# Attention's wide exponential cut into 1536 and 512 columns, and the normalisation's VectorE steps moved one behind each score copy

## The chip, the cores and the metric

The kernel runs on one core of one Trainium2 chip. The time is the device time of one execution in microseconds (us); before the change it is 2981.12 us, the median of three runs (2979.9 to 2981.21). The core's engines run side by side and wait for one another by semaphores: TensorE (PE in the profile; PEld are its weight loads), VectorE (DVE), ScalarE (ACT), GpSimd (POOL) and SyncE (SP), which issues most DMAs.

## What is computed

Two kinds of layers take turns, each on a layer norm of x and added to x: a long convolution (S4) and attention. x is 2048 x 640, all in float32. The change touches attention alone, which has 32 heads of 20 channels, all with the same keys and values:

```python
q = (x @ wq).reshape(B, S, H, Dh)        # S 2048, H 32, Dh 20, heads moved ahead of rows
k = x @ wk
v = x @ wv
scores = einsum("bhqd,bkd->bhqk", q, k) * Dh ** -0.5
p = softmax(scores, axis=-1)
o = einsum("bhqk,bkd->bhqd", p, v)
y = o.reshape(B, S, H * Dh) @ wo
...
x = x + A(layernorm(x)); x = x + B(layernorm(x))
x = x + A(layernorm(x)); x = x + B(layernorm(x))
```

## The kernel before

`attn_layer` runs twice (layers b and d); nearly all of its time is `main_loop`, whose work is cut into 1024 tiles. A tile is 128 keys by 1024 columns: 256 queries of four heads. Tiles run over four blocks of 512 queries (nb), in each over eight groups of four heads (hg), in each over two halves of the queries (f) and 16 blocks of keys (t), so 32 tiles make one (nb, hg).

What happens to a tile:

- **scores** (L1298): two matmuls on TensorE into a PSUM tile of two banks, of which there are three (`ps2`, tag s2).
- **the exponential** on ScalarE, in one of two ways. A *direct* tile goes from PSUM to SBUF (pt, L1304, 1024 columns). Two tiles of six are put *aside*: VectorE copies their scores to SBUF (L1311, the score copy), two of them side by side in a tile pw, and ScalarE later takes both in one *wide* exponential of 2048 columns in place (L1429).
- **values** (L1321): matmuls with the values, the probabilities as moving data, which add up over the 16 blocks of keys in one PSUM bank (po). The values have a column of ones, so the softmax's denominators come out as a row of the same sums.

After 32 tiles VectorE *normalises*: it copies the bank to SBUF (on, L1347), transposes (L1336), takes the reciprocal of the denominators (L1337) and transposes back (L1338), and multiplies (L1352); then SP sends the parts of on to chunks ot of 128 channels (L1358). The banks for values are two, s10 and s11, and (nb, hg) uses the one of hg % 2. The other is free for the **projection** (L1393): one eighth of one chunk times wo, which VectorE adds to x (L1380). A layer has some 150 projections in the loop; they are let in by a credit of 0.52 per half cycle.

TensorE, ScalarE and VectorE work in the order in which the code is written (`tc.manual_schedule`), and DMAs in the order of their queue. The loop goes in cycles c of six tiles. A cycle first lets ScalarE take the wide exponential of tiles c and c + 1, then has two halves (h). Each half issues three scores (a *burst*: one direct, one aside, one direct), then one of VectorE's waiting pieces, then, in `behind`, the values of three tiles three to one places back and perhaps a projection. In the first half these are the last three direct tiles of the cycle before, in the second the two put aside and the first direct one. ScalarE's order in a cycle is so: wide, direct, direct, direct, direct.

The order before for the normalisation: the copy of the bank and the first transposition follow the last of the 32 tiles' values at once, in `behind`; the other two pieces come one each in the next two halves. In a half whose last tile is tile 0 or 1 of a new (nb, hg), there is no projection, since its bank is still being copied; a finished chunk's projections may start from tile 15 on.

Of the kernel before, what the change touches and what calls it, by code (L numbers as in the profile page):

```python
# [15 lines left out]
AF = mybir.ActivationFunctionType  # L16
# [19 lines left out]
SCALE = 20.0**-0.5  # L36
# [159 lines left out]
class Net:  # L196
# [1065 lines left out]
    def main_loop(self, ap, mp, kt, vt, nm, out):  # L1262
# [10 lines left out]
        tc, nc, qps = self.tc, self.nc, self.qps  # L1273
# [5 lines left out]
        def late_loads(late):  # L1279
            nc.gpsimd.memset(wol, 0.0)  # L1280
            for j in range(4):
                nc.gpsimd.dma_start(wol[32 * j : 32 * j + 20],
                                    self.ins["B_wo"][20 * (28 + j) : 20 * (29 + j)])
            if out is None:
                self.conv_weights(nc.gpsimd, late)
# [3 lines left out]
        queue, later = [], []  # L1289

        def scores(i):
            nb, hg, f, t = tiles[i]
            if (nb, hg) not in qps:
                self.load_q(ap, nm, nb, hg)
            sc = self.ps2(f"sc{nm}{i}")
            for par in range(2):
                rows = slice(64 * par, 64 * par + 62)
                nc.tensor.matmul(sc[:, 512 * par : 512 * par + 512], kt[rows, 128 * t : 128 * t + 128],  # L1298
                                 qps[nb, hg][rows, f].rearrange("p a c -> p (a c)"), start=True, stop=True)
            return sc  # L1300
# [12 lines left out]
        def values(i):  # L1313
            nb, hg, f, t = tiles[i]
            if (nb, hg) not in pos:
                pos[nb, hg] = self.ps1(f"po{nm}{nb}{hg}", hg % 2)
            po, pt = pos[nb, hg], pts.pop(i)

            for j in range(4):
                c0 = 512 * (j % 2) + 256 * (j // 2)  # L1320
                nc.tensor.matmul(po[32 * j : 32 * j + 32, 256 * f : 256 * f + 256], vt[:, t],  # L1321
                                 pt[:, c0 : c0 + 256], start=(t == 0), stop=(t == 15))

        def chunk(nb, k):
            if (nb, k) not in ots:
                ots[nb, k] = mp.tile([P, 512], F32, tag=f"ot{k}", bufs=2, name=f"ot{nb}{k}")
                if (nb, k) == (3, 4):

                    nc.gpsimd.memset(ots[nb, k], 0.0)
            return ots[nb, k]  # L1330

        def inverses(den, name):

            tr = mp.tile([P, 16, 32], F32, tag="tr", bufs=1, name=f"tr{name}")
            rc = mp.tile([P, 16], F32, tag="rc", bufs=2, name=f"rc{name}")
            steps = [lambda: nc.vector.transpose(flat(tr), den),  # L1336
                     lambda: (nc.vector.reciprocal(rc, tr[:, :, 20]),  # L1337
                              nc.vector.transpose(flat(tr), rc[:, :, None].to_broadcast([P, 16, 32])))]  # L1338
            return flat(tr), steps

        def flat(a):
            return a.rearrange("p a b -> p (a b)")

        def normalize(nb, hg):
            po = pos.pop((nb, hg))
            on = mp.tile([P, 512], F32, tag="on", bufs=2, name=f"on{nb}{hg}")
            nc.vector.tensor_copy(on, po)  # L1347
            inv, steps = inverses(on, f"{nb}{hg}")
            steps[0]()

            def finish():
                nc.vector.tensor_tensor(on, on, inv, ALU.mult)  # L1352
                for j in range(4):
                    r = 20 * (4 * hg + j)
                    while r < 20 * (4 * hg + j) + 20:
                        e = min(20 * (4 * hg + j) + 20, (r // 128 + 1) * 128)
                        o = 32 * j + r - 20 * (4 * hg + j)
                        nc.sync.dma_start(chunk(nb, r // 128)[r % 128 : r % 128 + e - r], on[o : o + e - r])  # L1358
                        r = e
                for k in range(80 * hg // 128, 80 * (hg + 1) // 128):  # L1360
                    later.extend((nb, k, u) for u in range(8))

            pieces.extend([steps[1], finish])

        def normalize_last():

            po = pos.pop((3, 7))
            inv, steps = inverses(po, "l")
            for call in steps:
                call()  # L1370
            on = mp.tile([P, 512], F32, tag="on", bufs=2, name="onl")
            nc.vector.tensor_tensor(on, po, inv, ALU.mult)
            return on
# [15 lines left out]
        def product(py, o, w, u, m, start, stop, c0=0, n=320):  # L1389
            i, half = u // 2, u % 2  # L1390
            c0 += 320 * half
            for j in range(0, P, m):
                nc.tensor.matmul(py[j : j + m], o[:, 128 * i + j : 128 * i + j + m], w[:, c0 : c0 + n],  # L1393
                                 start=start, stop=stop)

        def projection(hg):

            nb, k, u = queue.pop(0)
            py = self.ps1(f"py{nm}{nb}{k}{u}", 1 - hg % 2)[:, 0:320]
            product(py, ots[nb, k], wo[:, k], u, 32, True, True)  # L1400
            add(nb, u, py, k == 4)

        n = len(tiles)
        credit, pieces = [0.0], []

        def behind(group):

            for i in group:
                values(i)
                if i % 32 == 31 and i + 1 < n:  # L1410
                    normalize(*tiles[i][:2])
            if not group:
                return
            if group[-1] % 32 >= (15 if group[-1] < n - 32 else 8):
                queue.extend(later)
                later.clear()
            credit[0] = min(credit[0] + 0.52, 1.5)
            if queue and credit[0] >= 1 and group[-1] % 32 not in (0, 1):
                credit[0] -= 1
                projection(tiles[group[-1]][1])  # L1420

        with tc.manual_schedule(engines={mybir.EngineType.PE, mybir.EngineType.Activation,
                                         mybir.EngineType.DVE}):
            for i, put in ((0, direct), (6, aside), (1, direct)):
                put(i, scores(i))
            for c in range(0, n, 6):
                w = wide.pop(c // 6, None)
                if w is not None:
                    nc.scalar.activation(flat(w), flat(w), AF.Exp, scale=SCALE)  # L1429
                for h in range(2):  # L1430
                    burst = [(c + 2 + 2 * h, direct), (c + 7 + 5 * h, aside), (c + 3 + 2 * h, direct)]
                    for i, put in burst:
                        if i < n:
                            put(i, scores(i))
                    if pieces:
                        pieces.pop(0)()
                    if c == 36 and h == 0:
                        late_loads(pts[38])
                    behind([i for i in range(c - 3 + 3 * h, c + 3 * h) if 0 <= i < n])
            behind([n - 1])  # L1440
            on = normalize_last()
            if out is None:
                self.norm("c", 0)

            last = []
            for g in range(3):
                tile_ = self.ps2(f"pl{nm}{g}")
                last += [tile_[:, 0:320], tile_[:, 512:832]]
            last.append(self.ps1(f"pl{nm}6", 0)[:, 0:320])
            last.append(self.ps1(f"pl{nm}7", 1)[:, 0:320])  # L1450
            left = queue + later
            for u in range(8):
                items = [(ots[nb, k], wo[:, k]) for nb, k, v in left if v == u and k < 4]
                items.append((ots[3, 4], wo[:, 4]))
                for n, (o, w) in enumerate(items):
                    product(last[u], o, w, u, P, n == 0, False)
            for u in range(0, 8, 2):
                for v in (u, u + 1):
                    product(last[v], on, wol, v, P, False, True)
                for v in (u, u + 1):  # L1460
                    add(3, v, last[v], True)
# [83 lines left out]
```

## Time and profile before

| | us |
|---|---|
| median of three runs | 2981.12 |
| the profiled execution | 2978.3 |
| its span, first to last instruction | 2976.4 |
| attention loop of layer b, about | 729 to 1664 |
| attention loop of layer d, about | 2024 to 2958 |

| engine, whole span | busy us | share |
|---|---|---|
| TensorE | 2733.0 | 92% |
| ScalarE | 2414.1 | 81% |
| VectorE | 2027.1 | 68% |

The two loops are 1869 of the 2976 us. In the loops all three engines work at once, and an instruction's record in the profile can overlap with the next one's on the same engine: the durations of a group don't add up to the time that the engine needs, the distances between starts do. A row of the timeline is: start, us from start to end, engine, line, operation, what it writes and reads, shapes, count; in brackets the idle time before it and who ended that. In names pob and pod are banks of values in layers b and d, scb and scd their score tiles, pyb and pyd the projections' sums, pld the last products behind the loop. In a row of stages (from:to, length) stand the busy time and count of PE, PEld, DVE, ACT, POOL, then the granted TensorE clock, the DMA engines' share and GB/s.

### The profile page before, as it was taken

How to read it: one execution, taken by the hardware profiler on the slowest of the kernel's cores; microseconds unless marked ns; L12 is line 12 of the kernel's file. 1: busy time of each engine (PE TensorE's matmuls, PEld its weight loads, DVE VectorE, ACT ScalarE, POOL GpSimd, SP SyncE). 2: the span in 40 equal slices, each digit the busy share in tenths (PEclk: the TensorE clock that was granted, in tenths of full speed). 3: DMA queues.
4: the chain of work that ended last, by engine and by line, in shares of the span. 5: the costliest groups of instructions: out<-in, count | busy, mean ns of one | idle time of the engine just before them, and what ended most of it. 6: DMA issues, size and time to landing. Idle time of an engine off the chain costs nothing. (4 is left out here: it accounts for less than half of the span.)

```text
span 2976.4 us, 69802 instructions
## 1 busy us (share of the span) xinstructions
PE 2733.0 (92%) x29940; PEld 1570.6 (53%) x29940; DVE 2027.1 (68%) x2486; ACT 2414.1 (81%) x2565; POOL 84.9 (3%) x140
## 2 busy tenths in 40 slices
PE   2776989898999999999999998998999999999999
PEld 0333978775444444444444687774444444444444
DVE  7999899943566666666666699725566656666655
ACT  5888243454999999999999734338999999999997
POOL 0000001100000000000000011000000000000000
PEclk9655999998999999999999999999999999999999
DMA  6114555533200010101010256231001101110100
GB/s 146 34 17 103 183 167 114 139 104 104 82 23 27 22 26 22 28 21 28 23 27 20 88 114 161 65 128 43 22 27 31 35 23 32 35 28 23 44 20 24
DMA packets 144184, 178.81 MB, mean 60 GB/s; under 512 B 59524, under 2 KB 115844, under 8 KB 140244
## 3 DMA queue, kind: packets, MB, share of 16 engines
q1 hardware_dynamic: 119704, 141.90, 16.2%
q0 software_dynamic: 21872, 30.69, 5.6%
q8 instruction: 239, 3.92, 0.6%
q10 hardware_dynamic: 2288, 1.64, 0.2%
q14 instruction: 81, 0.66, 0.1%
HBM read 95.22 MB, written 48.04 MB: 48 GB/s over the span
## 5 line engine op out<-in xcount | busy, mean ns | idle before, releaser
L1304 ACT ACTIVATE pt<-scb 128x1024 f32<-128x1024 f32 x684 | 653.5, 1046 | 14.3 <-PE scb L1298 7.2
L1304 ACT ACTIVATE pt<-scd 128x1024 f32<-128x1024 f32 x684 | 652.5, 1044 | 12.7 <-PE scd L1298 7.2
L1429 ACT ACTIVATE pw<-pw 128x2048 f32<-128x2048 f32 x340 | 657.3, 1933 | 0.0
L1311 DVE COPY pw<-scd 128x1024 f32<-128x1024 f32 x340 | 415.4, 1222 | 218.1 <-PE scd L1298 215.0
L1311 DVE COPY pw<-scb 128x1024 f32<-128x1024 f32 x340 | 414.8, 1220 | 212.4 <-PE scb L1298 206.9
L1298 PE MATMUL scb<-qpb,kt 62*128 62x512 f32 x2048 | 378.6, 449 | 27.1 <-ACT pt L1304 17.7
L1298 PE MATMUL scd<-qpd,kt 62*128 62x512 f32 x2048 | 379.5, 449 | 24.4 <-ACT pt L1304 15.7
L1321 PE MATMUL pob<-pt,vt 128*32 128x256 f32 x5472 | 363.4, 383 | 0.1
L1321 PE MATMUL pod<-pt,vt 128*32 128x256 f32 x5472 | 362.9, 383 | 0.1
L1298 PEld LDWEIGHTS scb<-qpb,kt 62*128 62x128 f32 x2048 | 170.4, 186 | 260.9 <-ACT pt L1304 163.7
L1298 PEld LDWEIGHTS scd<-qpd,kt 62*128 62x128 f32 x2048 | 170.0, 185 | 259.7 <-ACT pt L1304 163.8
L1321 PEld LDWEIGHTS pob<-pt,vt 128*32 128x32 f32 x5472 | 160.6, 110 | 152.0 <-issue 63.9
L1321 PEld LDWEIGHTS pod<-pt,vt 128*32 128x32 f32 x5472 | 160.5, 110 | 152.0 <-issue 63.9
L1321 PE MATMUL pod<-pw,vt 128*32 128x256 f32 x2720 | 182.0, 385 | 1.0 <-DVE x L1380 1.0
L1321 PE MATMUL pob<-pw,vt 128*32 128x256 f32 x2720 | 182.0, 385 | 1.0 <-DVE x L1380 1.0
L1380 DVE TENSOR_TENSOR x<-pyd,x 128x320 f32<-128x320 f32 x149 | 72.6, 487 | 144.0 <-PE pyd L1393 144.0
L1380 DVE TENSOR_TENSOR x<-pyb,x 128x320 f32<-128x320 f32 x149 | 72.7, 488 | 141.0 <-PE pyb L1393 141.0
L1321 PEld LDWEIGHTS pob<-pw,vt 128*32 128x32 f32 x2720 | 71.1, 109 | 74.1 <-issue 42.4
L1321 PEld LDWEIGHTS pod<-pw,vt 128*32 128x32 f32 x2720 | 71.1, 109 | 73.3 <-issue 41.6
L1393 PE MATMUL pyb<-wo,ot 128*32 128x320 f32 x1192 | 107.5, 432 | 0.5 <-DMA ot<-on 0.5
L1393 PE MATMUL pyd<-wo,ot 128*32 128x320 f32 x1192 | 107.5, 432 | 0.4 <-DMA ot<-on 0.4
L654 PE MATMUL zc<-xnc,wf 128*128 128x256 f32 x384 | 87.4, 391 | 4.6 <-ACT xnc L821 4.5
(378 smaller groups left out, 3559.4 us busy)
## 6 DMA issues: line engine op xcount, KB each, us to landing
Akh<-kh SPq DMA_DIRECT2D x10, 2048.0 KB
kh<-Ak SPq DMA_DIRECT2D x5, 2048.0 KB
qhd<-qh SPq DMA_DIRECT2D x40, 256.0 KB
qld<-ql SPq DMA_DIRECT2D x40, 256.0 KB
qpb<-qhd SPq DMA_DIRECT2D x256, 40.0 KB
qpd<-qhd SPq DMA_DIRECT2D x256, 40.0 KB
ot<-on SPq DMA_DIRECT2D x216, 40.0 KB
wi<-in_c_wi SPq DMA_DIRECT2D x16, 512.0 KB
```

What stands on the lines that cost most here:

```text
L654: nc.tensor.matmul(zv[:, :, c, kk], self.wf[:, t + 4 * h, j, c, kk], x, start=(n == 0), stop=(n == 3))
L1298: nc.tensor.matmul(sc[:, 512 * par : 512 * par + 512], kt[rows, 128 * t : 128 * t + 128], qps[nb, hg][rows, f].rearrange("p a c -> p (a c) ...
L1304: nc.scalar.activation(pts[i], sc, AF.Exp, scale=SCALE)
L1311: nc.vector.tensor_copy(pts[i], sc)
L1321: nc.tensor.matmul(po[32 * j : 32 * j + 32, 256 * f : 256 * f + 256], vt[:, t], pt[:, c0 : c0 + 256], start=(t == 0), stop=(t == 15))
L1380: nc.vector.tensor_tensor(xh, py, xh, ALU.add)
L1393: nc.tensor.matmul(py[j : j + m], o[:, 128 * i + j : 128 * i + j + m], w[:, c0 : c0 + n], start=start, stop=stop)
L1429: nc.scalar.activation(flat(w), flat(w), AF.Exp, scale=SCALE)
```

## The change

The wide exponential is cut: columns 0 to 1535 are taken where the whole was, ahead of the first half's burst, and the last 512 ahead of the second half's, so between the second and the third direct one. The copy of the bank no longer follows the last values; it and the first transposition become pieces of their own, so that a normalisation is four pieces, one in each of the next four halves, each behind that half's score copy. While a bank waits to be copied (`unread`) there is no projection, whatever the tile's number. A chunk's projections start from tile 17 (14 in the layer's last 32 tiles) in place of 15 (8).

```diff
         def normalize(nb, hg):
             po = pos.pop((nb, hg))
             on = mp.tile([P, 512], F32, tag="on", bufs=2, name=f"on{nb}{hg}")
-            nc.vector.tensor_copy(on, po)
             inv, steps = inverses(on, f"{nb}{hg}")
-            steps[0]()
+            unread.append(po)
+
+            def read():
+                nc.vector.tensor_copy(on, unread.pop())
...
-            pieces.extend([steps[1], finish])
+            pieces.extend([read] + steps + [finish])
...
-        credit, pieces = [0.0], []
+        credit, pieces, unread = [0.0], [], []
...
-            if group[-1] % 32 >= (15 if group[-1] < n - 32 else 8):
+            if group[-1] % 32 >= (17 if group[-1] < n - 32 else 14):
...
-            if queue and credit[0] >= 1 and group[-1] % 32 not in (0, 1):
+            if queue and credit[0] >= 1 and not unread:
...
             for c in range(0, n, 6):
                 w = wide.pop(c // 6, None)
-                if w is not None:
-                    nc.scalar.activation(flat(w), flat(w), AF.Exp, scale=SCALE)
                 for h in range(2):
+                    if w is not None:
+                        cols = flat(w)[:, 1536 * h : 1536 + 512 * h]
+                        nc.scalar.activation(cols, cols, AF.Exp, scale=SCALE)
                     burst = [(c + 2 + 2 * h, direct), (c + 7 + 5 * h, aside), (c + 3 + 2 * h, direct)]
```

In the rows below a number behind a name tells buffers' generations apart; the lines of the changed file are three or four higher behind the edited places (L1429 becomes L1433, L1393 becomes L1395, L1380 L1382, L1347 L1351, L1352 L1354).

ScalarE in the middle of a loop, before (pt are direct tiles, pw the wide ones):

```order
L1304 ACTIVATE pt_20157<-scb_20154 128x1024
L1304 ACTIVATE pt_20166<-scb_20163 128x1024
L1304 ACTIVATE pt_20194<-scb_20191 128x1024
L1304 ACTIVATE pt_20204<-scb_20201 128x1024
L1429 ACTIVATE pw_20134<-pw_20134 128x2048
L1304 ACTIVATE pt_20225<-scb_20222 128x1024
L1304 ACTIVATE pt_20234<-scb_20231 128x1024
```

and now:

```order
L1433 ACTIVATE pw_20847<-pw_20847 128x1536
L1304 ACTIVATE pt_20954<-scb_20951 128x1024
L1304 ACTIVATE pt_20963<-scb_20960 128x1024
L1433 ACTIVATE pw_20847<-pw_20847 128x512
L1304 ACTIVATE pt_20987<-scb_20984 128x1024
L1304 ACTIVATE pt_20997<-scb_20994 128x1024
L1433 ACTIVATE pw_20931<-pw_20931 128x1536
```

One instruction per cycle is added, and a quarter of the wide one's columns has moved behind two direct tiles.

VectorE around a normalisation in layer b, before (pw the score copies, on the bank's copy, x the sum of a projection):

```order
L1311 COPY pw_11707<-scb_11732 128x1024 [waits PE_49]
L1347 COPY on_11753<-pob_11430 128x512 [waits DMAHW6_49,DMAHW5_49,DMAHW7_49,DMAHW4_49,PE_49]
L1336 STREAM_TRANSPOSE tr_11755<-on_11753 128x512 [waits DVE_49]
L1380 TENSOR_TENSOR x<-pyb_11758,x 128x320 [waits PE_49]
L1311 COPY pw_11772<-scb_11769 128x1024 [waits PE_49,Activation_49]
L1337 RECIPROCAL rc_11756<-tr_11755 128x16 [waits DVE_49]
L1338 STREAM_TRANSPOSE tr_11755<-rc_11756 128x512 [waits DVE_49]
L1311 COPY pw_11772<-scb_11800 128x1024 [waits PE_49]
L1352 TENSOR_TENSOR on_11753<-on_11753,tr_11755 128x512 [waits DVE_49]
```

and at the same normalisation now:

```order
L1311 COPY pw_11716<-scb_11747 128x1024 [waits PE_49]
L1311 COPY pw_11780<-scb_11777 128x1024 [waits DVE_49,PE_49,Activation_49]
L1351 COPY on_11768<-pob_11438 128x512 [waits DMAHW6_49,DMAHW7_49,DMAHW5_49,DMAHW4_49]
L1382 TENSOR_TENSOR x<-pyb_11801,x 128x320 [waits PE_49]
L1311 COPY pw_11780<-scb_11813 128x1024 [waits PE_49]
L1336 STREAM_TRANSPOSE tr_11769<-on_11768 128x512 [waits DVE_49]
L1311 COPY pw_11844<-scb_11841 128x1024 [waits PE_49,Activation_49]
L1337 RECIPROCAL rc_11770<-tr_11769 128x16 [waits DVE_49]
L1338 STREAM_TRANSPOSE tr_11769<-rc_11770 128x512 [waits DVE_49]
L1382 TENSOR_TENSOR x<-pyb_11865,x 128x320 [waits PE_49]
L1311 COPY pw_11844<-scb_11877 128x1024 [waits PE_49]
L1354 TENSOR_TENSOR on_11768<-on_11768,tr_11769 128x512 [waits DVE_49]
```

The copy of the bank has moved behind the next score copy and no longer waits for TensorE, and the multiply stands two score copies later.

TensorE in that half of the changed kernel:

```order
L1298 MATMUL scb_11777<-qpb_11635,kt 128x512 [waits DVE_49]
L1298 MATMUL scb_11777<-qpb_11635,kt 128x512
L1298 MATMUL scb_11782<-qpb_11635,kt 128x512 [waits Activation_49]
L1298 MATMUL scb_11782<-qpb_11635,kt 128x512
L1321 MATMUL pob_11788<-pw_11655,vt 32x256 x5
L1321 MATMUL pob_11788<-pw_11655,vt 32x256 [waits Activation_49]
L1321 MATMUL pob_11788<-pw_11655,vt 32x256 x2
L1321 MATMUL pob_11788<-pt_11745,vt 32x256 x4
L1395 MATMUL pyb_11801<-wo,ot_11217 32x320 [waits DVE_49,PE_49]
L1395 MATMUL pyb_11801<-wo,ot_11217 32x320 x3
L1298 MATMUL scb_11808<-qpb_11635,kt 128x512 [waits Activation_49]
```

Two waits are new: the sixth of the eight value matmuls on the two tiles put aside waits for ScalarE (the 512 columns), and the projection waits for VectorE, whose copy of the same bank is in the rows above.

## The prediction

> **What bounds the kernel now.** I read the busy times of the whole page first, then the busy time of each engine by stage, then ScalarE's order of time inside attention's loop.
>
> ```profile
> PE 2733.0 (92%) x29940; PEld 1570.6 (53%) x29940; DVE 2027.1 (68%) x2486; ACT 2414.1 (81%) x2565; POOL 84.9 (3%) x140
> PE 28%; ACT 3%; issue 1%; DVE 0%; DMA 0%; ACTq 0%; SPq 0%; DVEq 0%
> 729.00:1664.00 935.00, 914.62 (x11362) 435.71 (x11358) 577.92 (x675) 929.58 (x848) 5.69 (x17) 1.00 0.10 28
> 2024.00:2958.00 934.00, 915.52 (x11367) 435.62 (x11362) 567.44 (x639) 929.26 (x848) 6.90 (x13) 1.00 0.10 27
> ```
>
> The chain of waits and the whole page name TensorE, but the change touches only the two loops of the last two rows. There ScalarE (fourth busy time of a row) is busy 929.58 of 935.00 us and 929.26 of 934.00, at a granted clock of 1.00. TensorE's 98% counts modelled ends of pipelined matmuls. So I ask how short a cycle of six tiles could be on ScalarE.
>
> ```profile
> 742.11 3.81 ACT L1304 ACTIVATE pt<-scb 128x1024 f32<-128x1024 f32 x4
> 745.73 2.00 ACT L1429 ACTIVATE pw<-pw 128x2048 f32<-128x2048 f32 x1
> 747.53 3.86 ACT L1304 ACTIVATE pt<-scb 128x1024 f32<-128x1024 f32 x4
> 751.14 2.04 ACT L1429 ACTIVATE pw<-pw 128x2048 f32<-128x2048 f32 x1
> L1429 ACT ACTIVATE pw<-pw x170: 1903/1915/2062, 729.3 to 1661.9; 128x2048 f32<-128x2048 f32 x170
> L1429 ACT ACTIVATE pw<-pw x170: 1906/1915/2056, 2024.6 to 2955.7; 128x2048 f32<-128x2048 f32 x170
> ```
>
> Records overlap, so the price of an instruction is the distance to the next start, not its duration. The wide exponential takes 747.53 - 745.73 = 1.80 us, four direct ones 751.14 - 747.53 = 3.61 us (0.90 each): an undisturbed cycle is 5.41 us. The 169 cycles between the first and the last wide one took 932.6 us and 931.1 us, against 169 x 5.41 = 914.3. **All that ScalarE loses in both loops is 18.3 + 16.8 = 35.1 us**: the most that a better order can win.
>
> **Where the 35.1 us are.** The rows of a cycle with a projection, and of one with two:
>
> ```profile
> 1202.51 1.96 ACT L1429 ACTIVATE pw<-pw 128x2048 f32<-128x2048 f32 x1
> 1204.31 3.85 ACT L1304 ACTIVATE pt<-scb 128x1024 f32<-128x1024 f32 x4
> 1208.04 1.92 ACT L1429 ACTIVATE pw<-pw 128x2048 f32<-128x2048 f32 x1
> ...
> 2097.34 2.08 ACT L1304 ACTIVATE pt<-scd 128x1024 f32<-128x1024 f32 x2
> 2099.89 1.94 ACT L1304 ACTIVATE pt<-scd 128x1024 f32<-128x1024 f32 x2 [0.47 <-PE scd L1298]
> ```
>
> In the first, four direct ones take 3.73 us, 0.12 more than 3.61. In the second, the third direct one starts 2.55 us after the first in place of 1.81, 0.74 late, and the releaser is TensorE's score. The third direct one is the place: its score comes behind three tiles of values, and behind a projection if there is one.
>
> **Part 1, the split: what it costs.** 340 wide exponentials become 340 of 1536 and 340 of 512 columns. No row of before has these sizes from SBUF, so I take the distances of starts of other sizes:
>
> ```profile
> 51.85 1.04 ACT L436 ACTIVATE s<-f 128x1024 f32<-128x1024 f32 x1
> 52.79 1.13 ACT L437 ACTIVATE c<-fa,halfpi 128x1024 f32<-128x1024 f32 x1
> ...
> 552.04 0.40 ACT L1050 ACTIVATE wh<-kv 128x260 fp32r<-128x260 f32 x1
> 552.35 0.72 ACT L1050 ACTIVATE wh<-xnas 128x640 fp32r<-128x640 f32 x1
> 552.98 0.51 ACT L694 ACTIVATE xnas<-x 128x384 f32<-128x384 f32 x1
> ...
> 615.31 0.57 ACT L1181 ACTIVATE qh<-pqb 128x512 fp32r<-128x512 f32 x1
> 615.79 0.57 ACT L1182 ACTIVATE qs<-pqb 128x512 fp32r<-128x512 f32 x1
> ```
>
> From SBUF, 260 columns take 0.31 us, 640 take 0.63, 1024 take 0.94 and 2048 take 1.80. From the first to the last that is 1.49 us for 1788 columns, 0.833 ns each, which leaves 0.31 - 0.217 = 0.093 us fixed; 640 and 1024 lie on the same line. From PSUM, 512 take 0.48 and 1024 take 0.90: about 0.05 us fixed. The price from below is 0 (1.80 us cut in proportion), from above 0.18 us (what the records of 260 and 1024 columns, 0.40 and 1.04 us, leave at none, if they did not overlap; the starts above show that they do). I take 0.093, since four sizes from the same memory lie on that line: 1.373 + 0.520 against 1.80, or **340 x 0.093 = +31.6 us**, on the engine that is the bound. The floor of a cycle becomes 5.50 us.
>
> The Trainium skill, "ScalarE: Activation LUTs", section "What ACT_TABLE_LOAD costs", gives an ACTIVATE with immediates 186 ns + 0.833 ns a column, and says that back-to-back ones overlap by about 93 ns. An estimate from it is 31.6 us with the overlap and 63.2 us without, a total of +39 us. It makes no difference by memory, and would put a direct one at 0.946 us, where the rows show 0.90: there the row decides.
>
> **Part 1, what it wins.** The third direct one may now come 0.52 us later after the second, and a cycle has 0.09 us more: 0.61 us of lateness that costs nothing. The 0.12 us of the common cycle are gone, the 0.74 us shrink to 0.13. So nearly all of the 35.1 us go, and I credit them whole and charge below what stays. TensorE keeps up:
>
> ```profile
> 1203.28 0.97 PE L1298 MATMUL scb<-qpb,kt 62*128 62x512 f32 x6
> 1204.18 1.50 PE L1321 MATMUL pob<-pt,vt 128*32 128x256 f32 x24
> 1205.61 1.23 PE L1298 MATMUL scb<-qpb,kt 62*128 62x512 f32 x6
> 1206.77 1.07 PE L1321 MATMUL pob<-pw,vt 128*32 128x256 f32 x16
> 1207.66 0.61 PE L1321 MATMUL pob<-pt,vt 128*32 128x256 f32 x8
> 1208.09 0.72 PE L1393 MATMUL pyb<-wo,ot 128*32 128x320 f32 x8
> 1208.74 0.51 PE L1298 MATMUL scb<-qpb,kt 62*128 62x512 f32 x2
> ```
>
> A cycle with one projection is 5.46 us here, of which the scores from 1205.61 took 1.16 to the values, where those from 1203.28 took 0.90: 0.26 us is a wait for ScalarE. Its own need is 5.20, under 5.50. The values now wait for the 512 columns too. These would start 0.90 us after the second direct one (1204.31 + 0.90) and, with the 0.1 us by which records outlast distances, end at 1206.73; the first value is at 1206.77 and the one that needs them is the sixth, so the wait is over.
>
> **Part 2, VectorE's pieces.** They keep their durations, and VectorE has room (577.92 of 935.00). But the copy out of the values' bank now runs behind the next score copy, and a projection of that half, which uses the same bank, waits for it.
>
> ```profile
> 1204.06 1.23 DVE L1311 COPY pw<-scb 128x1024 f32<-128x1024 f32 x1 [0.15 <-PE scb L1298]
> 1206.46 1.23 DVE L1311 COPY pw<-scb 128x1024 f32<-128x1024 f32 x1 [1.17 <-PE scb L1298]
> L1347 DVE COPY on<-pob 128x512 f32<-128x512 f32 x31 | 21.3, 688 | 7.2 <-PE pob L1321 6.3 <-DMA qpb<-qhd 0.9
> L1352 DVE TENSOR_TENSOR on<-on,tr 128x512 f32<-128x512 f32 x31 | 21.1, 682 | 0.0
> ```
>
> In a second half the score copy would end at 1207.69 and the bank's copy at 1208.38, 0.29 us after the projection's 1208.09. In a first half they end at 1205.29 and 1205.98, 0.48 after 1205.50, where a projection would start (three tiles of values at 0.44 behind 1204.18). With 0.1 us of hand-over, as between values and scores (1205.50 to 1205.61), TensorE waits 0.4 and 0.6. Behind the waiting projection stand the next half's scores, and ScalarE waits for those. By the order of the change each layer has 25 such projections (8 copies in all were followed by one in their half before, 50 now): 17 in second halves, 8 in first. What reaches ScalarE is the lateness over 0.61 us. A second half alone has 0.12 + 0.4: nothing. The 6 per layer that have a projection in the next half too have 0.74 + 0.4 - 0.61 = 0.53; the 8 first halves 0.12 + 0.6 - 0.61 = 0.11; the 5 other pairs per layer 0.13. Both layers: 12 x 0.53 + 16 x 0.11 + 10 x 0.13 = **+9.4 us**. From below this is 0, from above 34 x 0.4 + 16 x 0.6 + 1.3 = 24.5 if no slack covers them.
>
> The last piece, the multiply, comes two halves later, and so do its DMAs, on SP; the first projection that reads a chunk stands two halves behind that piece.
>
> ```profile
> 2938.71 3.75 SPq L1358 DMA_DIRECT2D ot<-on  x5
> 2939.47 2.07 DMA ot<-on
> ```
>
> SP needs 0.75 us for each issue and a transfer 2.07, so the third, the last that such a chunk needs, lands 4.3 us after the piece. The projection comes 5.0 us after it (piece until 1205.29 + 0.68, projection at 1205.61 + 3.13 + 2.22 = 1210.96): nothing. Without that cover it would be some 0.5 us for each of 22 chunks, inside the high end.
>
> **The ends of the loops.** The last rows of the second loop; the first ends alike:
>
> ```profile
> 2955.74 1.91 ACT L1429 ACTIVATE pw<-pw 128x2048 f32<-128x2048 f32 x1
> 2957.53 1.94 ACT L1304 ACTIVATE pt<-scd 128x1024 f32<-128x1024 f32 x2
> ...
> 2958.78 1.38 PE L1321 MATMUL pod<-pt,vt 128*32 128x256 f32 x16
> 2959.98 0.72 PE L1393 MATMUL pyd<-wo,ot 128*32 128x320 f32 x8
> 2960.63 6.19 PE L1393 MATMUL pld<-wo,ot 128*128 128x320 f32 x22
> ```
>
> Now the 512 columns come last on ScalarE, about when the last direct one ended (2955.74 + 1.37 + 1.80 + 0.61 = 2959.52 against 2959.47), and behind them stand three tiles of values, less the first groups (1.3 us at 0.44 a tile), where there was one: +0.9. One projection per layer moves out of the loop (149 become 148), two more rows of 6.19/22 = 0.28 us: +0.55. Two layers: **+2.9 us**, from below 0 if other work of the end hides it.
>
> **Sum**, on the profiled execution (span 2976.4 us, time 2978.3): +31.6 - 35.1 + 9.4 + 2.9 = **+8.8 us**, 2987.1. The runs' median is 2981.12, 2.8 above that execution; on it the forecast is **2989.9 us**, slower by 0.3%.
>
> **Rivals.** (1) *The split is free*: ScalarE hides the fixed 0.093 us of the short piece, and only the wins stay. The slack is then 0.45 us, so 10 pairs keep 0.29, 12 keep 0.69, the 16 first halves 0.27 and the 22 second halves alone 0.07, 17 us in all: 17 + 2.9 - 35.1 = -15, **2966 us, faster**. The point from which the change gains is a cut that costs under (35.1 - 9.4 - 2.9)/340 = 0.067 us. For it: three quarters of the wide one keep their long stretch. Against it: no row from SBUF lies under the line, and 260 columns pay as much as 640. The Trainium skill, "Perfetto Trace Analysis", section "Optimizing Scalar/DVE Operations", has a rule on each side: to break up instructions where ScalarE isn't saturated but causes bubbles elsewhere, and to group them where it is; 929.58 of 935.00 us busy is the second case, which would give the forecast; by the first the time would be near this rival's.
>
> (2) *The waits all vanish and the ends hide*: 31.6 - 35.1 = -3.5, 2977.6, or with the ends -0.6, **2980.5 us, no change**. For it: the releasers of ScalarE's idle time are scores only, and what I charge for the projections behind the copies rests on a few tenths of slack.
>
> (3) *The copies behind bind*: each of the 50 projections holds TensorE and no slack covers it: 31.6 - 35.1 + 24.5 + 2.9 = +23.9, **3005 us**. For it: VectorE's copy, 1.23 + 0.69 us behind a score that itself waits for a buffer. Against it: TensorE has 0.3 us to spare in every cycle.
>
> **How the numbers follow.** My forecast and its surroundings (2984 to 2996) get 0.55, rival 2 0.26, rival 3 0.13, rival 1 0.06. The range runs from 2977.6 (rival 2 without the ends) to 3003, just short of rival 3's full price, and leaves out rival 1. About 0.2%, 6 us, is what a measurement here can tell from no change: rival 2 and 0.09 of the forecast's 0.55 (below 2987) fall within it, 0.35; faster is 0.06, slower 0.59.
>
> **What would show it.** After: the start of the 1536 columns to the next start 1.37 us, of the 512 columns 0.52; four direct and two pieces at 5.50 us in most cycles; no idle time of ScalarE before the third direct one except in pairs of projections, some 10 to 22 per layer; in the waits, projections of TensorE released by VectorE's copy of the bank, some tenths each; first to last wide start about 936 us in a layer. The prediction is wrong in its main term if the two distances add up to 1.80 us, and in its second if scores or projections make ScalarE wait in many more cycles than those counted.

## The result and the profile after

The change takes 2996.92 us (median of four runs) against 2980.51 before: +16.4 us, a ratio of 1.0057 with a 95% interval of 1.0044 to 1.007. It is slower, as forecast, by nearly twice the +8.8 us that were forecast; the time lies in the stated range (2977.6 to 3003), just above the forecast's own surroundings (2984 to 2996). The profiled execution's span is 2993.5 us against 2976.4, +17.1. Of all the executions below one, of the run with cuts only where ScalarE waits longest, took 5125.67 us, for a reason that stays open, and its ratio leaves it out.

The whole page's busy times and chain of waits, after:

```profile
PE 2730.7 (91%) x29928; PEld 1562.9 (52%) x29928; DVE 2027.4 (68%) x2484; ACT 2437.4 (81%) x2905; POOL 84.9 (3%) x140
PE 17%; ACT 11%; issue 4%; DVE 0%; DMA 0%; ACTq 0%; DVEq 0%; SPq 0%
```

ScalarE has 340 instructions and 23.3 us of busy time more. Of the chain of work that ended last, TensorE's share has fallen from 28% to 17% and ScalarE's has risen from 3% to 11%. What each loop waits for is read from ScalarE's rows below.

ScalarE's wide exponentials, by line (durations in ns, first and last start in us), of layers b and d:

```profile
L1433 ACT ACTIVATE pw<-pw x340: 632/1330/2045, 729.2 to 1672.2; 128x1536 f32<-128x1536 f32 x170
L1433 ACT ACTIVATE pw<-pw x340: 633/1332/2040, 2031.7 to 2974.4; 128x1536 f32<-128x1536 f32 x170
```

The last start is now that of a 512-column piece, 3.18 us (1.37 and two direct ones) behind the last 1536. So the 169 cycles took 943.0 - 3.2 = 939.8 us and 942.7 - 3.2 = 939.5 us, where before they took 932.6 and 931.1: +15.6 us, nearly all of the 17.1.

ScalarE in order of time, a stretch without projections:

```profile
740.32 1.54 ACT L1433 ACTIVATE pw<-pw 128x1536 f32<-128x1536 f32 x1
741.69 2.00 ACT L1304 ACTIVATE pt<-scb 128x1024 f32<-128x1024 f32 x2
743.50 0.71 ACT L1433 ACTIVATE pw<-pw 128x512 f32<-128x512 f32 x1
744.02 2.01 ACT L1304 ACTIVATE pt<-scb 128x1024 f32<-128x1024 f32 x2
745.83 1.58 ACT L1433 ACTIVATE pw<-pw 128x1536 f32<-128x1536 f32 x1
747.20 2.03 ACT L1304 ACTIVATE pt<-scb 128x1024 f32<-128x1024 f32 x2
...
751.33 1.62 ACT L1433 ACTIVATE pw<-pw 128x1536 f32<-128x1536 f32 x1
```

The distances of the pieces are those that were forecast: 741.69 - 740.32 = 1.37 and 744.02 - 743.50 = 0.52. But look at the second column: from cycle to cycle the same instruction's record is 0.04 us longer (1.54, 1.58, and 1.62 one later). The starts come every 5.51 us (740.32 to 745.83), the ends every 5.55 (741.86 to 747.41). **The starts run ahead of the ends, by more in each cycle.** The rows of before in the prediction show the same: the four direct ones at 742.11 end at 745.92, those at 747.53 at 751.39, 5.47 apart, where the prediction read 5.41 from the starts. So, against what is said ahead of the prediction, the distances of starts don't add up to the engine's time either: in such a stretch they are too short. In the undisturbed cycles of the whole loops the ends are 5.455 us apart before and 5.545 after.

Measured by ends, 169 cycles need 921.9 us before and 937.1 after. The loops before lost 10.7 and 9.2 us over that, 19.9 together and not 35.1; after they lose 2.7 and 2.4. So: +30.4 us for the second piece (338 cycles of 0.09), -14.8 us of waits that went, +15.6 in the loops, and 1.5 outside them.

### The profile page after: what moved, and what is told of

It reads as the page before. It is cut to its first block, busy times and chain, and to the rows that moved or that the text cites. A ratio compares the mean times of both kernels' runs of the same rounds, so it can differ in the third digit from the quotient of the medians.

```text
span 2993.5 us, 70134 instructions
## 1 busy us (share of the span) xinstructions
PE 2730.7 (91%) x29928; PEld 1562.9 (52%) x29928; DVE 2027.4 (68%) x2484; ACT 2437.4 (81%) x2905; POOL 84.9 (3%) x140
## 5 line engine op out<-in xcount | busy, mean ns | idle before, releaser
L1433 ACT ACTIVATE pw<-pw 128x1536 f32<-128x1536 f32 (+1 forms) x680 | 853.2, 1255 | 0.0
L1304 ACT ACTIVATE pt<-scd 128x1024 f32<-128x1024 f32 x684 | 728.9, 1224 | 9.4 <-DMA qpd<-mxd 4.5
L1304 ACT ACTIVATE pt<-scb 128x1024 f32<-128x1024 f32 x684 | 717.1, 1189 | 10.2 <-PE scb L1298 8.6
L1298 PE MATMUL scd<-qpd,kt 62*128 62x512 f32 x2048 | 371.9, 447 | 31.0 <-ACT pt L1304 17.0
L1298 PE MATMUL scb<-qpb,kt 62*128 62x512 f32 x2048 | 370.4, 446 | 31.4 <-ACT pt L1304 17.9
L1382 DVE TENSOR_TENSOR x<-pyd,x 128x320 f32<-128x320 f32 x148 | 72.7, 491 | 140.9 <-PE pyd L1395 139.9
L1382 DVE TENSOR_TENSOR x<-pyb,x 128x320 f32<-128x320 f32 x148 | 72.8, 492 | 137.7 <-PE pyb L1395 136.7
L1395 PE MATMUL pyb<-wo,ot 128*32 128x320 f32 x1184 | 107.8, 434 | 5.6 <-DVE on L1351 3.3
L1395 PE MATMUL pyd<-wo,ot 128*32 128x320 f32 x1184 | 107.8, 434 | 3.8 <-DVE on L1351 2.0
```

The costliest lines, as they stand in the source:

```text
L1304: nc.scalar.activation(pts[i], sc, AF.Exp, scale=SCALE)
L1382: nc.vector.tensor_tensor(xh, py, xh, ALU.add)
L1433: nc.scalar.activation(cols, cols, AF.Exp, scale=SCALE)
```

## The experiments

Each time is a median, beside the median of before on the same chip. Times of loops come from one profiled execution of each run. "Loss" is what a layer's 169 cycles take over ScalarE's own pace, 921.9 us uncut and 937.1 cut.

### The cut without VectorE's part

```diff
-                if w is not None:
-                    nc.scalar.activation(flat(w), flat(w), AF.Exp, scale=SCALE)
                 for h in range(2):
+                    if w is not None:
+                        cols = flat(w)[:, 1536 * h : 1536 + 512 * h]
+                        nc.scalar.activation(cols, cols, AF.Exp, scale=SCALE)
```

> The wide exponential is cut and its 512 columns moved as in the change; the normalisation and the conditions for projections are those of before. Theory A (ScalarE's own pace sets the loops: by the distances between the ends of its records 5.455 us a cycle uncut and 5.545 cut): from first to last wide start 937.1 us a layer at least, 937 to 942 in the run, so +15 us or so in total, within 4 us of the whole change. Rival B (the copies of the bank behind the score copies, and projections held by them, cost a good part of the +16 us): 6 us or more below the whole change, under 936 us a layer.

2993.58 against 2980.97 us, +12.6, ratio 1.0041 (1.0027 to 1.0055). The wide pieces, both layers:

```profile
L1431 ACT ACTIVATE pw<-pw x340: 633/1380/2144, 730.9 to 1672.4; 128x1536 f32<-128x1536 f32 x170
L1431 ACT ACTIVATE pw<-pw x340: 633/1348/2062, 2032.1 to 2973.2; 128x1536 f32<-128x1536 f32 x170
```

Less 3.2 us, 938.3 and 937.9 us: about 1 us of loss each. ScalarE hardly ever waits, and the kernel is still 12.6 us slower. Theory A holds and rival B falls. VectorE's part adds 3.1 us to the two loops of the change (1879.3 us against 1876.2); the totals, +16.4 and +12.6 with intervals that overlap, don't tell the two kernels apart.

### VectorE's part without the cut

The change with its two lines of the cut put back to the single `activation` of before, ahead of `for h in range(2)`.

> VectorE's four pieces and the new conditions for projections as in the change; the wide exponential whole, at the start of the cycle, as before. Theory A: floor 921.9 us a layer; without the slack that the cut gives, the waits of projections behind the copy of the bank reach ScalarE, so loops of 932 to 942 us a layer, total 0 to +18 us against before. Rival B (the pieces alone cost what the change costs): +14 to +18 us. Rival C (the pieces make the score copies earlier and win): loops under 930 us a layer, total -4 us or less.

3000.40 against 2980.97 us, +19.4, ratio 1.0063 (1.0046 to 1.008). Its wide exponentials:

```profile
L1431 ACT ACTIVATE pw<-pw x170: 1903/1917/2055, 731.9 to 1674.9; 128x2048 f32<-128x2048 f32 x170
L1431 ACT ACTIVATE pw<-pw x170: 1903/1917/2058, 2038.0 to 2977.6; 128x2048 f32<-128x2048 f32 x170
```

TensorE's waits ahead of the weight loads of layer b's projections (us in total, times, longest):

```profile
PEld pyb L1395 <- issue: 15.4, 24, 1.3
```

The loops take 943.0 and 939.6 us, a loss of 21.1 and 17.8. That is 1 us over theory A's range in one layer and within it in the other; the total is 1.4 us above its range and also above rival B's. VectorE's part by itself costs about as much as the whole change, or a little more; rival C falls. The two parts don't add up (12.6 + 19.4 against 16.4). TensorE waits ahead of its projections in the change too (17.6 us in layer b, the row stands further down), but with the cut little of that reaches ScalarE.

### VectorE's part, with no projection beside the copy

```diff
-            if queue and credit[0] >= 1 and not unread:
+            if queue and credit[0] >= 1 and not unread and not held:
...
+                    held[:] = unread
                     if pieces:
                         pieces.pop(0)()
```

> As pieces_only (whole wide exponential, VectorE's pieces and conditions of the change), but no projection either in the half in which the bank is copied. Theory A (the pieces cost by projections that wait for the copy of their bank): TensorE's projections and their weight loads wait no more for the copy (in pieces_only 15.4 and 13.8 us a layer of issue waits before them, 0.9 in before); what the loops lose over 921.9 us falls from 21.1 and 17.8 us to 9 to 14 a layer, the pairs of projections being 11 a layer as before. Rival E (the later place of the pieces on VectorE is what costs): the loss stays over 17 us a layer.

2982.60 against 2980.43 us, +2.2, ratio 1.0007 (0.9998 to 1.0016).

```profile
L1431 ACT ACTIVATE pw<-pw x170: 1904/1915/2058, 731.6 to 1665.3; 128x2048 f32<-128x2048 f32 x170
L1431 ACT ACTIVATE pw<-pw x170: 1903/1916/2059, 2028.3 to 2959.9; 128x2048 f32<-128x2048 f32 x170
```

The waits ahead of the projections are gone from the list, and the loss is 11.8 and 9.7 us, as theory A had it. What VectorE's part cost was the projections held by the copy of their bank; the later place of the pieces on VectorE costs nothing that these runs show. Nor is it the number of pairs: a projection in a first half with one in the half before comes 11 times a layer in this run and in the one before it alike (7 in the kernel before the change).

### The cut without the move

```diff
                 if w is not None:
-                    nc.scalar.activation(flat(w), flat(w), AF.Exp, scale=SCALE)
+                    for cols in (flat(w)[:, 0:1536], flat(w)[:, 1536:2048]):
+                        nc.scalar.activation(cols, cols, AF.Exp, scale=SCALE)
```

> Before, with the wide exponential cut into 1536 and 512 columns at the same place, one right behind the other; nothing is moved. Theory A: 340 x 0.09 = +30 us on ScalarE, less what cycles in which ScalarE waits for TensorE absorb: total +22 to +31 us, loops of 943 to 948 us a layer. Rival D (a cut costs nothing by itself; the change lost by the move): 0 to +3 us.

3002.08 against 2980.97 us, +21.1, ratio 1.0068 (1.0051 to 1.0084). The wide pieces, both layers:

```profile
L1430 ACT ACTIVATE pw<-pw x340: 618/1126/1632, 731.0 to 1676.2; 128x1536 f32<-128x1536 f32 x170
L1430 ACT ACTIVATE pw<-pw x340: 617/1128/1634, 2036.8 to 2980.9; 128x1536 f32<-128x1536 f32 x170
```

Here the last start is 1.4 us behind the last 1536, so the loops take 943.8 and 942.7 us. The profiled execution is 24.0 us longer than before's. That is theory A, with the total and one loop just under its low end, and rival D falls. A second piece costs this much where nothing else moves, and the move wins a part of it back: the loops of the cut that is moved are 10 us shorter in all.

### The cut in four

```diff
                 if w is not None:
-                    nc.scalar.activation(flat(w), flat(w), AF.Exp, scale=SCALE)
+                    for q in range(4):
+                        cols = flat(w)[:, 512 * q : 512 * q + 512]
+                        nc.scalar.activation(cols, cols, AF.Exp, scale=SCALE)
```

> Before, with the wide exponential in four pieces of 512 columns at the same place. Theory A: three more pieces of 0.09 us in each of 340 cycles, 92 us, less what was lost before (20 us at most): total +75 to +92 us, the median cycle by ends 5.73 us. Rival D (the loss of the cut is something of the two pieces, such as the odd length): not in proportion, under +60 us.

One execution: 3056.86 us, +76.4 against the median of before. ScalarE in order of time:

```profile
901.21 2.33 ACT L1431 ACTIVATE pw<-pw 128x512 f32<-128x512 f32 x4
903.29 3.91 ACT L1304 ACTIVATE pt<-scb 128x1024 f32<-128x1024 f32 x4
906.95 2.32 ACT L1431 ACTIVATE pw<-pw 128x512 f32<-128x512 f32 x4
```

Four pieces take 2.08 us where the whole took 1.80: 0.28 for three more, 0.09 each, and by ends (903.54 and 909.27) a cycle is 5.73 us. The price goes by the number of pieces, which rival D denied.

### ScalarE's own pace

In the function `projection`, the product and its addition are left out for the first three blocks of queries:

```diff
             nb, k, u = queue.pop(0)
+            if k == 4 and u % 2:
+                ...
+            if nb < 3:
+                return
```

> Before, without the projections of the first three blocks of queries inside the loops (their products and their additions to x are left out), so that TensorE has 0.65 us less to do in most cycles and ScalarE is never kept waiting there. Theory A: those cycles take 5.455 us each on the mean (the pace of ScalarE's ends). The floor of the prediction: 5.41 us (the distances between starts).

Its time (2966.17 us, one execution) compares with nothing, since work is missing. ScalarE, with no wait of its own:

```profile
887.40 2.06 ACT L1438 ACTIVATE pw<-pw 128x2048 f32<-128x2048 f32 x1
889.20 3.92 ACT L1304 ACTIVATE pt<-scb 128x1024 f32<-128x1024 f32 x4
892.86 2.05 ACT L1438 ACTIVATE pw<-pw 128x2048 f32<-128x2048 f32 x1
894.66 3.92 ACT L1304 ACTIVATE pt<-scb 128x1024 f32<-128x1024 f32 x4
898.31 2.05 ACT L1438 ACTIVATE pw<-pw 128x2048 f32<-128x2048 f32 x1
```

Here the record of the wide one no longer grows (2.05, 0.14 over its 1.91 behind a wait), and the starts come at 5.46 and 5.45 us too: four direct ones are 3.66 or 3.65 apart, not 3.61. Once the starts are as far ahead as they get, they show the pace of the ends. That is theory A's 5.455; the prediction's 5.41 falls.

### Cuts only where ScalarE waits longest

But for the last cycle of each loop, the longest waits of before are those of the 14 cycles whose first half and the half before it both hold a projection (a pair).

```diff
-                if w is not None:
-                    nc.scalar.activation(flat(w), flat(w), AF.Exp, scale=SCALE)
+                cut = pair(c - 1)
                 for h in range(2):
+                    if w is not None and (h == 0 or cut):
+                        cols = flat(w)[:, 1536 * h : 1536 + 512 * h if cut else 2048]
+                        nc.scalar.activation(cols, cols, AF.Exp, scale=SCALE)
```

(`pair` says whether the half before had a projection and this one will.)

> Before, with the wide exponential cut (1536 and 512 columns, placed as in the change) in 14 cycles alone: those in which the half before and the first half both hold a projection, 7 a layer. Theory A (each cut costs ScalarE 0.09 us, and wins what it waits for TensorE there, some 0.55 us each by the distances between ends): loops 3.2 us a layer shorter than before's 932.6 and 931.1, total -6 us, some 2974 us. Rival D (cuts cost nothing, or the waits would come back elsewhere): the waits come back, total 0 within 2 us.

2980.81 against 2980.43 us, ratio 1.0001 (0.9992 to 1.001). Nothing is won: theory A's -6 us is a miss, and the time is what rival D had for waits that come back. ScalarE in such a cycle of layer d, in before (its first direct ones stand in the prediction) and here:

```profile
2095.53 2.05 ACT L1429 ACTIVATE pw<-pw 128x2048 f32<-128x2048 f32 x1
...
2099.89 1.94 ACT L1304 ACTIVATE pt<-scd 128x1024 f32<-128x1024 f32 x2 [0.47 <-PE scd L1298]
2101.71 1.91 ACT L1429 ACTIVATE pw<-pw 128x2048 f32<-128x2048 f32 x1
```

```profile
2097.36 1.63 ACT L1437 ACTIVATE pw<-pw 128x1536 f32<-128x1536 f32 x1
2098.85 1.98 ACT L1304 ACTIVATE pt<-scd 128x1024 f32<-128x1024 f32 x2
2100.67 0.67 ACT L1437 ACTIVATE pw<-pw 128x512 f32<-128x512 f32 x1
2101.71 1.94 ACT L1304 ACTIVATE pt<-scd 128x1024 f32<-128x1024 f32 x2 [0.37 <-PE scd L1298]
```

The third direct one still waits. It starts 4.35 us behind the wide one (before: 2099.89 - 2095.53 = 4.36): its moment is set by TensorE, and the 512 columns only changed places with time ahead of them. In the 14 cycles the third direct one's loss by ends is 0.47 us on the mean, 0.55 in before.

### Cuts in the cycles ahead

So a cut would have to help TensorE earlier: with 512 columns less ahead of it, the second direct exponential of its cycle ends 0.43 us sooner, and that frees a score buffer for which TensorE waits. Against the kernel of the last experiment (`pair` is gone too):

```diff
-                cut = pair(c - 1)
+                cut = any(0 < p - c <= 18 for p in (84, 222, 318, 660, 756, 852, 990))
```

(42 cuts, in the three cycles ahead of the 14; the 14 themselves are whole.)

> Before, with the wide exponential cut in the three cycles ahead of each of the 14 cycles in which the half before and the first half both hold a projection, and whole in those cycles themselves. Theory F (a cut wins in later cycles: it lets the second direct exponential of its own cycle end 0.43 us earlier, with it the score that waits for its bank, so that TensorE gets ahead by up to 0.2 us a cycle): in the 14 cycles the loss over 5.455 us falls from 0.55 to under 0.25; 42 cuts cost 3.8 us, so total -3 to +1 us. Rival G (a cut wins only in its own cycle): the loss there stays at 0.5 to 0.6, total about +4 us.

2976.57 against 2979.13 us, ratio 0.999 (0.998 to 0.9999). The same cycle:

```profile
2095.45 2.14 ACT L1432 ACTIVATE pw<-pw 128x2048 f32<-128x2048 f32 x1
2097.25 4.07 ACT L1304 ACTIVATE pt<-scd 128x1024 f32<-128x1024 f32 x4
2101.21 1.92 ACT L1432 ACTIVATE pw<-pw 128x2048 f32<-128x2048 f32 x1
```

No idle time, and 5.76 us from wide to wide where before has 6.18 (2095.53 to 2101.71). The mean loss of the third direct one in the 14 cycles is 0.09 us. Theory F holds, rival G falls; the total itself is barely clear of no change. TensorE's weights for the last score ahead of the pair, in before and here, show the buffer:

```profile
2094.02 0.19 PEld L1298 LDWEIGHTS scd<-qpd,kt 62*128 62x128 f32 x2 [0.73 <-ACT pt L1304]
```

```profile
2093.51 0.18 PEld L1298 LDWEIGHTS scd<-qpd,kt 62*128 62x128 f32 x2 [0.62 <-ACT pt L1304]
```

Both wait for a direct exponential. In before the load comes 3.94 us behind the start of its cycle's wide one (2090.08), here 3.56 us behind the start of the 1536 columns (2089.95).

### The pairs taken away

```diff
-            credit[0] = min(credit[0] + 0.52, 1.5)
+            credit[0] = min(credit[0] + 0.52, 1.47)
```

A half behind one with a projection then has at most 0.47 + 0.52 = 0.99 of credit, so no half holds one if the half before it did. Put into before:

> Before, with the credit's cap at 1.47 in place of 1.5, so that no two halves in a row hold a projection; nothing is cut. Theory A: the 14 long waits of ScalarE go without a price on ScalarE, -7.7 us in the loops; two projections more per layer behind the loop, +2.2 us; total -5 us, some 2975 us. Rival (the waits come from something else than the pair of projections): loops within 1 us of before.

2971.94 against 2980.43 us, -8.5, ratio 0.9971 (0.9959 to 0.9983): **faster than before and than the change**.

```profile
L1429 ACT ACTIVATE pw<-pw x170: 1903/1915/2059, 730.1 to 1658.3; 128x2048 f32<-128x2048 f32 x170
L1429 ACT ACTIVATE pw<-pw x170: 1904/1915/2057, 2020.8 to 2946.9; 128x2048 f32<-128x2048 f32 x170
```

928.2 and 926.1 us: 9.4 us less in the loops than before, a little more than theory A had, and the rival falls. The same line put into the change:

> The change, with the credit's cap at 1.47 in place of 1.5, so that no two halves in a row hold a projection. Theory A (what the change loses is ScalarE's price for the second piece, not TensorE's waits): loops at ScalarE's pace of 937.1 us a layer within 2 us, some 2 us less than the change in both layers together, and some more work behind the loops: total +12 to +17 us against before. Rival B (the pairs behind a copied bank are what makes the change slow): within 4 us of no_pairs, which was 8 us faster than before.

2995.00 against 2979.13 us, +15.9, ratio 1.005 (1.0033 to 1.0067).

```profile
L1433 ACT ACTIVATE pw<-pw x340: 632/1342/2061, 728.1 to 1669.4; 128x1536 f32<-128x1536 f32 x170
L1433 ACT ACTIVATE pw<-pw x340: 637/1342/2069, 2030.3 to 2971.2; 128x1536 f32<-128x1536 f32 x170
```

Less 3.2 us, its loops take 938.1 and 937.7 us, within 1 us of ScalarE's pace: rival B falls. With almost no wait left, the change is still slower than before, since its pieces cost more (30.4 us) than all the waits that before has to lose (19.9).

## Why the prediction came out as it did

The direction was right, and so was the main cost: ScalarE is the engine that the loops wait for, and each cut adds about 0.09 us to it. The rows after have the two distances that were named, 1.37 and 0.52 us; the pace by ends puts the price at 30.4 us, the forecast at 31.6. But the balance was another than forecast. In the prediction the cuts by themselves won a little more than they cost (31.6 - 35.1), and only the charges for what stays and for the ends, 9.4 and 2.9 us, made the kernel slower. In the runs the price alone outweighs all that could be won: 30.4 - 19.9 + 5.1 + 1.5 = 17.1 us. The credit was too large by 15.2 us and the other three terms by 6.9 in all, so the errors partly cancelled. That the time lies in the range is in part luck: the upper part of the range was there for copies that bind, which aren't the cause.

**The step that was off is the credit of 35.1 us**, "all that ScalarE loses in both loops", credited whole. It was 169 cycles against a floor of 5.41 us read from the distances of starts. The pace of the ends is 5.455 us, so 15.2 of those 35.1 us were never idle, and only 19.9 could go. The run without projections shows the floor by itself. 14.8 us went. The same step put the first to last wide start at about 936 us in a layer after, where the runs have 939.8 and 939.5. The prediction had warned that records overlap and durations are no price; it took the next thing, the starts, for the pace, and the lengthening records stood in its own quoted rows.

**What stays of the waits** was charged at 9.4 us; by ends the loops keep 5.1. Of these, 3.5 us go when the pairs are taken away (loops of 938.1 and 937.7 us) and 3.1 when VectorE's part is (938.3 and 937.9), so pairs behind copies make up most of it, as they did in the charge. The mechanism is there: in the change the cycle of a copy in a first half reads (TensorE's values, VectorE's copies, the projection, the next scores, ScalarE's third direct one):

```profile
1378.81 1.94 ACT L1433 ACTIVATE pw<-pw 128x1536 f32<-128x1536 f32 x1
1378.95 0.98 PE L1298 MATMUL scb<-qpb,kt 62*128 62x512 f32 x6
1379.73 1.23 DVE L1311 COPY pw<-scb 128x1024 f32<-128x1024 f32 x1 [1.40 <-PE scb L1298]
1379.86 1.50 PE L1321 MATMUL pob<-pt,vt 128*32 128x256 f32 x24
...
1380.87 0.68 DVE L1351 COPY on<-pob 128x512 f32<-128x512 f32 x1
1381.65 0.74 PE L1395 MATMUL pyb<-wo,ot 128*32 128x320 f32 x8 [0.29 <-issue]
...
1381.99 1.11 ACT L1433 ACTIVATE pw<-pw 128x512 f32<-128x512 f32 x1
...
1382.33 0.97 PE L1298 MATMUL scb<-qpb,kt 62*128 62x512 f32 x6
...
1382.93 1.99 ACT L1304 ACTIVATE pt<-scb 128x1024 f32<-128x1024 f32 x2
...
1384.75 1.54 ACT L1433 ACTIVATE pw<-pw 128x1536 f32<-128x1536 f32 x1
```

and the waits ahead of the projections' weight loads in layer b:

```profile
PEld pyb L1395 <- issue: 17.6, 28, 1.7
```

Values from 1379.86 would let the projection start at 1381.18; it starts at 1381.65, behind the copy's end at 1381.55: 0.5 us late, for which 0.6 was forecast. The 28 waits of layer b are 0.6 us each on the mean. ScalarE's third direct one starts 0.94 us behind the 512 columns in place of 0.52, but what it gives up is the lead of the starts over the ends: by ends (1380.75 to 1386.29) this cycle takes 5.54 us and loses nothing.

**The values' wait for the 512 columns** cost nothing inside the loops, as forecast, and came at their ends. The group of layer b's values on the tiles put aside, from the page:

```profile
L1321 PE MATMUL pob<-pw,vt 128*32 128x256 f32 x2720 | 182.6, 385 | 1.0 <-ACT pw L1433 1.0
```

Its 1.0 us is one wait, at 1672.90, behind the loop's last 512 columns. What lies outside the loops grew by 1.5 us where the forecast had 2.9.

**The rivals.** The free split fell: the cut in place and the cut in four show the price. No change fell with the credit. The copies that bind would explain a time above the forecast, but are not the cause: the cut without VectorE's part is slower by 12.6 us, and the change without pairs by 15.9. (With the other terms as they stand, the price of 63.2 us that the prediction works out beside its own gives +40.4 us in place of +39; nothing rests on it.) **Where the cut wins** was told only in part: the prediction had the third direct one's lateness covered in its own cycle. The cuts in the 14 cycles alone won nothing and those in the cycles ahead did, so the room comes from a score buffer that is freed earlier in the cycles before. The change, with a cut in every cycle, has both.

What stays open: why the starts can run ahead of the ends, and up to where; and which of the cycles after the change only give up lead and which lose time was read from their ends, not tried by itself.

## What to carry to other kernels

Before crediting an engine's idle time, find its pace where nothing keeps it waiting, from the ends of its records over several cycles, and look whether the same instruction's record grows from cycle to cycle. On an engine that is the bound, an instruction cut in two costs its fixed part (here 0.09 us) once more at every pass, and a better order has to win that back first. Where a few places in a loop make it wait, look at what makes those places different (here two projections in a row) before paying everywhere for room.

## What the runs showed that was not expected

ScalarE's starts can lead its ends by a growing amount. In the change the record of a 1536-column exponential grows from 1.50 to 2.04 us within 16 cycles and falls back where a start is held up; uncut, that of 2048 columns stops at 2.05, 0.14 us over its least. By ends a direct exponential of 1024 columns from PSUM takes 0.914 us, by starts 0.902.
